# Two collecting PSUM tiles begin without zero products, and the order of all engines is made anew

## The chip, the cores and the metric

The kernel runs on one core of one Trainium2 chip. The core has TensorE (products into PSUM, with weights loaded ahead of each product), VectorE, ScalarE and POOL (GpSimd), and queues that issue DMAs from SyncE, ScalarE and POOL. The metric is the device time of one execution in microseconds (us); less is better. Before the change it was 365.63 us, the median of 3 runs (365.37 to 367.65).

## The reference

`x` is 2048 x 512. A branch `a` takes the real two-dimensional FFT of `x`, multiplies by a complex filter and transforms back. A branch `b` is a dense layer with GELU and 1792 inner features. A gate for each row mixes them:

```python
g = sigmoid((x * gate_w).sum(-1, keepdims=True))
a = irfft2(rfft2(x) * (w_r + 1j * w_i))
b = gelu(x @ w1 + b1) @ w2 + b2
return g * a + (1 - g) * b
```

## The kernel before

All arithmetic is float32; a product that needs the full width is made of three: both operands are split into a high part and a low rest, and high x high, high x low and low x high are added in PSUM (`prods`).

The rows are dealt into four groups of 512, called columns 0 to 3. The FFT branch runs as a forward half (`forward`: TensorE folds, products pd with the table cf, then products py), radix-4 steps along the rows on VectorE (`stage1`, `filt`, `stage4`), the filter (products m with the table wf, in `filt`), and an inverse half (`inverse`: products pz, then pa). The dense branch works on the first half of the columns (`CA`, function `mlp`) as it stands: for each of 14 blocks of inner features, up products into a PSUM tile ph, GELU and a split into high and low part g on ScalarE and VectorE, then down products into po.

The second half of the columns (`CB`, function `fast`) uses a scheme with fewer products. It takes two blocks of features and two columns as a 2 x 2 product of matrices and forms it with seven combined products (function `times`, six matmuls each) in place of eight. Two of the four results are formed in PSUM tiles N, which are new for each pair of blocks. The others pass through the two collecting tiles X[0] and X[1] (ux0 and ux1 in the profile), which are made once and stay for the whole second half. ScalarE copies N[0] into X[0] (`copy`, line 1191), `times(X[0], ...)` then adds onto what stands there, and X[1] is filled by a copy of X[0] in the same way. The products that add onto X never carry the flag that starts an accumulation; before the change, one product of zeros with that flag was made into each collecting tile ahead of the first copy (lines 1166 to 1171).

What runs when is settled by a planner in the kernel file (class `Graph`). Every piece of work is a step: an engine, a cost, the buffers that it reads and writes, and a rank. `add` finds the dependencies; `schedule` plays the steps through time with the written costs, and whenever an engine is free it takes, of the steps whose inputs are there, the one with the lowest rank for which tiles are free. Tiles come from pools of fixed size (PSUM: two pools of four banks, `pf` and `pm`; SBUF: `w` with 46 tiles, `t2k` with 7, `ttab` with 3), tiles of one class are handed out in the order in which the steps were created, and some classes have a ceiling (`most`). The result is one fixed order of instructions for each engine and DMA queue; on the chip each engine runs its own list in that order and waits on semaphores for the others. The ranks are a list of numbers, `RANKS`, one for each step in the order of creation:

```python
ranks = RANKS.split()
assert len(ranks) == len(g.steps)
for s, r in zip(g.steps, ranks):
    s.rank = 0.05 * int(r)
order = g.schedule()
```

Names used below: xf, w, eo, pd, cf, py, zb (forward half); wf, m, y, b0..b3 and c0..c3 with d, s, u (radix steps and filter; y is the spectrum in place); pz, pa, od, u, v (inverse half); ph, g, po, o (dense branch, first half); nu, ux, five, g, poB, oB (second half; nu are the tiles N); wa, wb, ws are first- and second-layer weights, a trailing h or l is the high or low part. `bacc` in device memory collects the dense result: ScalarE takes a po tile out into o, and POOL issues DMAs that add it to bacc.

Line 507 is the helper that issues matmuls, line 1185 the matmuls of `times`, line 498 POOL's adding DMAs and line 558 the low parts of g.

Of the kernel before, what the change touches and what calls it, by code (L numbers as in the profile page):

```python
# [11 lines left out]
F32 = mybir.dt.float32  # L12
# [420 lines left out]
def tile_kernel(ctx: ExitStack, tc: tile.TileContext, xt, xc, w1, w2, b1, b2, x0g, wf, wrev, out, consts):  # L433
# [72 lines left out]
    def mm(ps, w, x, start, stop):  # L506
        pe.matmul(ps, w, x, start=start, stop=stop)  # L507
# [653 lines left out]
    def fast(p):  # L1161
# [4 lines left out]
        if p == 0:  # L1166
# [3 lines left out]
            for x in free["X"]:  # L1170
                m(lambda x=x: mm(x.ap(), zero.ap(), bcast(zero.ap(), 4), True, True), 512, 1, [zero], [x])
# [206 lines left out]
```

## Time and profile before

The profiled execution took 368.04 us of its own, with a span of 366.2 us from its first to its last instruction.

| | us | share of the span |
|---|---|---|
| median of 3 runs | 365.63 | |
| profiled execution | 368.04 | |
| its span | 366.2 | |
| VectorE (DVE) busy | 327.8 | 90% |
| ScalarE (ACT) busy | 256.7 | 70% |
| POOL busy | 69.6 | 19% |

TensorE is PE in the profile, its weight loads PEld. Matmuls are pipelined and the end of each is modelled, so the records of neighbours overlap; the distance from one start to the next is the time that a product holds the engine. TensorE's granted clock averaged 0.999 of full speed.

The share of the 16 DMA engines that were busy, and what they moved, in 40 equal slices of the span:

```profile
DMA  7999785647885937999999943339887637799896
GB/s 224 306 322 303 253 233 166 106 149 233 206 204 129 189 58 155 273 263 365 196 153 217 264 85 117 86 122 225 126 141 150 100 64 156 173 296 241 199 250 184
```

### The profile page before, as it was taken

How to read it: one execution, taken by the hardware profiler on the slowest of the kernel's cores; microseconds unless marked ns; L12 is line 12 of the kernel's file. 1: busy time of each engine (PE TensorE's matmuls, PEld its weight loads, DVE VectorE, ACT ScalarE, POOL GpSimd, SP SyncE). 2: the span in 40 equal slices, each digit the busy share in tenths (PEclk: the TensorE clock that was granted, in tenths of full speed). 3: DMA queues.
4: the chain of work that ended last, by engine and by line, in shares of the span. 5: the costliest groups of instructions: out<-in, count | busy, mean ns of one | idle time of the engine just before them, and what ended most of it. 6: DMA issues, size and time to landing. Idle time of an engine off the chain costs nothing.

```text
span 366.2 us, 5746 instructions
## 1 busy us (share of the span) xinstructions
PE 358.7 (98%) x1808; PEld 302.9 (83%) x1808; DVE 327.8 (90%) x746; ACT 256.7 (70%) x471; POOL 69.6 (19%) x89
## 2 busy tenths in 40 slices
PE   8999999999999999999999999999999999999994
PEld 8888898898878778878888788888888888888884
DVE  5999988998759999899999999999999769899962
ACT  4985778789986241753759975999999998655200
POOL 0210001100211311410333100002333112121220
PEclk9999999999999999999999999999999999999999
DMA  7999785647885937999999943339887637799896
GB/s 224 306 322 303 253 233 166 106 149 233 206 204 129 189 58 155 273 263 365 196 153 217 264 85 117 86 122 225 126 141 150 100 64 156 173 296 241 199 250 184
DMA packets 46719, 70.35 MB, mean 192 GB/s; under 512 B 5600, under 2 KB 19424, under 8 KB 46688
## 3 DMA queue, kind: packets, MB, share of 16 engines
q1 hardware_dynamic: 34880, 48.93, 41.8%
q0 software_dynamic: 11376, 20.71, 35.3%
q10 hardware_dynamic: 432, 0.33, 0.3%
q8 instruction: 14, 0.23, 0.3%
q14 instruction: 17, 0.14, 0.1%
HBM read 48.32 MB, written 19.41 MB: 185 GB/s over the span
## 4 chain that ended last, share of the span: by engine, by line
PE 75%; DVE 12%; DMA 5%; ACT 4%; issue 2%; SPq 1%; DVEq 0%; ACTq 0%
PE poB L507 20%; PE po L507 13%; PE ph L507 11%; PE ux L1185 9%; PE nu L1185 7%; PE pd L507 4%; PE pz L507 3%; PE py L507 3%; PE pa L507 3%; DVE m L856 3%; DMA wf<-in_wf 3%; DMA y<-ownr 1%; DMA xf<-in_xt 1%; DVE y L760 1%; DVE y L758 1%
## 5 line engine op out<-in xcount | busy, mean ns | idle before, releaser
L995 ACT ACTIVATE ph<-ph,b1t 128x512 f32<-128x512 f32 x28 | 18.4, 658 | 25.5 <-PE ph L507 25.2
L498 POOL DMA_DIRECT2D bacc<-o x16 | 15.3, 1029 | 43.2 <-ACT o L1073 43.2
L894 ACT ACTIVATE sw<-y,al 64x512 f32<-64x512 f32 x32 | 22.8, 718 | 0.6
L498 POOL DMA_DIRECT2D bacc<-oB x16 | 13.9, 889 | 43.0 <-ACT oB L1073 33.7
L856 DVE TENSOR_TENSOR m<-y,wf 128x514 f32<-128x514 f32 x32 | 20.7, 688 | 0.0
L507 PE MATMUL pd<-cf,w 128*128 128x129 f32 x128 | 17.7, 276 | 0.0
L507 PEld LDWEIGHTS pz<-tg,pq 128*128 128x128 f32 x128 | 16.8, 191 | 1.1
L507 PEld LDWEIGHTS pd<-cf,w 128*128 128x128 f32 x128 | 16.6, 191 | 1.2 <-DVE zb L698 0.3
L1185 PE MATMUL nu<-xf,wa0h 128*128 128x512 f32 x56 | 17.3, 390 | 0.0
L507 PE MATMUL pz<-tg,pq 128*128 128x128 f32 x128 | 17.2, 274 | 0.0
L507 PE MATMUL py<-zb,tf 128*128 128x258 f32 x96 | 17.1, 295 | 0.0
L723 ACT ACTIVATE y<-pys 64x257 f32<-64x257 f32 x32 | 13.2, 417 | 3.9 <-DVE pys L720 3.4
L507 PE MATMUL pa<-zb,ci 128*128 128x256 f32 x96 | 15.2, 285 | 0.2 <-ACT od L935 0.2
L507 PEld LDWEIGHTS pa<-zb,ci 128*128 128x128 f32 x96 | 13.8, 189 | 1.9 <-ACT od L935 0.7
L507 PEld LDWEIGHTS py<-zb,tf 128*128 128x128 f32 x96 | 14.1, 190 | 1.2 <-ACT pys L716 0.2
L1073 ACT ACTIVATE o<-po 128x512 f32<-128x512 f32 x16 | 9.2, 593 | 8.3 <-PE po L507 8.2
L901 DVE SCALAR_TENSOR_TENSOR pq<-y,al,sw 128x256 f32<-128x256 f32 x32 | 14.4, 479 | 0.0
L695 ACT ACTIVATE zb<-pd 128x256 fp32r<-128x256 f32 x32 | 11.6, 384 | 3.9 <-PE py L507 3.9
L698 DVE TENSOR_TENSOR zb<-pd,zb 128x256 fp32r<-128x256 f32 x32 | 12.5, 417 | 1.1 <-ACT zb L695 1.1
L665 DVE TENSOR_TENSOR w<-eo 128x256 f32<-128x256 f32 x32 | 12.8, 418 | 0.0
L662 DVE TENSOR_TENSOR eo<-xf 128x256 f32<-128x256 f32 x32 | 12.4, 419 | 0.0
L1185 PEld LDWEIGHTS nu<-xf,wa0h 128*128 128x128 f32 x56 | 10.5, 188 | 2.2
(701 smaller groups left out, 1274.3 us busy)
## 6 DMA issues: line engine op xcount, KB each, us to landing
wf<-in_wf SPq DMA_DIRECT2D x16, 257.0 KB, 4.7
bacc<-o POOLq DMA_DIRECT2D x16, 256.0 KB, 6.1
bacc<-oB POOLq DMA_DIRECT2D x16, 256.0 KB, 4.9
xf<-in_xt SPq DMA_DIRECT2D x14, 256.0 KB, 5.0
wr<-in_w SPq DMA_DIRECT2D x14, 256.0 KB, 4.9
tf<-tf SPq DMA_DIRECT2D x16, 192.0 KB, 2.8
bacc<-o SPq DMA_DIRECT2D x8, 256.0 KB, 3.2
ba<-bacc SPq DMA_DIRECT2D x8, 256.0 KB, 4.1
```

Of the source, the lines that this page charges most:

```text
L498: return add("pool", 2.3 * kb / 340, 3.4, lambda: nc.gpsimd.dma_start(dst(), src(), accum_op=ALU.add), reads, writes, rank)
L507: pe.matmul(ps, w, x, start=start, stop=stop)
L662: v(lambda s=s, op=op: vec.tensor_tensor(eo.ap()[:, s], x.ap()[:, 0:2], x.ap()[:, 2:4], op=op), 256, [x], [(eo, s)], feed)
L665: v(lambda s=s, op=op: vec.tensor_tensor(w.ap()[:, s], eo.ap()[:, :, 0], eo.ap()[:, :, 1], op=op), 256, [eo], [(w, s)], feed)
L695: a(lambda c=c: act.activation(segs(xh, c), both(c), AF.Copy), 256, [ps[c]], [(xh, c)], 0)
L698: v(lambda c=c: vec.tensor_tensor(segs(xl, c), both(c), segs(xh, c), op=ALU.subtract), 256, [ps[c], (xh, c)], [(xl, c)], 0)
L723: a(lambda o=o, i=i: act.activation(Y[j].ap()[o:o + HP, 1], pys.ap()[i:i + HP, 1], AF.Copy), 257, [(pys, 1)], [(Y[j], 1 + k)], 0, more=0.1)
L856: v(lambda mk=mk, k=k, y=y, w=w: vec.tensor_tensor(mk.ap(), y.ap(), w.ap()[:, k:k + 1, :ND].to_broadcast([P, 2, ND]), op=ALU.mult), 514, [ ...
L894: a(lambda sw=sw, y=y, o=o, i=i: act.activation(sw.ap()[o:o + HP], y.ap()[i:i + HP, ::-1, :HD], AF.Copy, scale=al.ap()[i:i + HP, 0:1]), 51 ...
L901: v(lambda sw=sw, pq_=pq_, y=y, j=j, k=k, op=op: vec.scalar_tensor_tensor(pq_.ap()[:, k], y.ap()[:, k, :HD], al.ap()[:, 1 + j:2 + j], sw.a ...
L995: a(lambda: act.activation(ps.ap(), ps.ap(), AF.Gelu_apprx_tanh, bias=b1t.ap()[:, f:f + 1]), 600, [b1t], [ps]).table = "gelu"
L1185: pe.matmul(o.ap(), w(wi, e), FX[j].ap()[:, xi, e], start=first, stop=k == 5, skip_group_check=not start)
```

## The change

The tile of zeros, its fill on VectorE and the two products into the collecting tiles are removed. The first access to X[0] and X[1] is now the copy by ScalarE, and the products that add onto them are as before. With three steps fewer (2013 in place of 2016) the list of ranks has a new length, and all its numbers are new. Nothing else differs: costs, pools, ceilings and the other steps are the same.

```diff
 RANKS = """
-0 12 294 321 326 399 330 333 323 340 343 1 13 7 14 20 23 11 35 26 10 2 5 8 19 4 32 56 47 53 78 22 42 73 43 45 21 25 72
...
-2003 2005 2004 2009 2008 2010 2006 2015
+24 7 37 65 66 76 80 81 82 86 72 4 16 3 18 27 0 14 56 43 6 13 10 1 5 12 40 47 93 21 91 42 71 92 70 28 17 32 118 108 106
...
+2008 2009 2010 2011 2012
 """
...
         late = [] if p else [free[CA[1]]]
         if p == 0:
             free["X"] = [buf("pm", [P, 512], F32, f"ux{k}", pool=pp, cls=f"ux{k}") for k in range(2)]
-            zero = buf("w", [P, P], F32R, "zerob", cls="zero")
-            add("vec", 0.3, 0.1, lambda: vec.memset(zero.ap().bitcast(F32), 0.0), [free[CA[1]]], [zero])
-            for x in free["X"]:
-                m(lambda x=x: mm(x.ap(), zero.ap(), bcast(zero.ap(), 4), True, True), 512, 1, [zero], [x])
         X = free["X"]
```

152 rows, old and new, of the table RANKS are left out of this document.

## The prediction

> **What bounds the kernel now.** The page comes first, for the busy shares; then the chain of waits, for what ends last; then the busy time by stretches, for where TensorE is ever idle.
>
> ```profile
> span 366.2 us, 5746 instructions
> PE 358.7 (98%) x1808; PEld 302.9 (83%) x1808; DVE 327.8 (90%) x746; ACT 256.7 (70%) x471; POOL 69.6 (19%) x89
> PE 75%; DVE 12%; DMA 5%; ACT 4%; issue 2%; SPq 1%; DVEq 0%; ACTq 0%
> ```
>
> TensorE is busy for 358.7 of 366.2 us and carries 75% of the chain. The stretches say where the rest is (first number after the stretch is its length, then TensorE, weight loads, VectorE):
>
> ```profile
> 0.00:13.40 13.40, 11.70 (x66) 10.77 (x67) 8.75 (x26) 8.07 (x15) 2.35 (x12) 1.00 0.82 267
> 13.40:101.00 87.60, 87.58 (x491) 75.41 (x489) 79.72 (x217) 72.12 (x154) 9.52 (x11) 1.00 0.79 221
> 101.00:164.70 63.70, 62.82 (x274) 50.69 (x273) 57.78 (x119) 33.05 (x56) 14.98 (x17) 1.00 0.81 181
> 164.70:205.00 40.30, 40.30 (x178) 33.23 (x179) 39.82 (x83) 27.50 (x52) 12.23 (x14) 1.00 1.02 236
> 361.50:366.30 4.80, 0.00 (x0) 0.00 (x0) 0.42 (x1) 0.00 (x0) 0.00 (x0) 0.90 0.51 149
> ```
>
> Before 13.4 us TensorE waits for the first loads; from 361.5 on it has finished and the last output leaves. Between these, its idle time is 0.02 us up to 101, then 0.88 us in the stretch to 164.7 where VectorE does the filter, and 0 in the stretch where the removed products stand. So the sum of the products sets the time, and what an order can win is small. How small follows from the chain's pieces, which give the spacing of products without a wait (start, us, what):
>
> ```profile
> 183.79 4.99 PE po L507 x22
> 188.78 0.23 PE ux L507
> 189.68 1.36 PE nu L1185 x6
> 191.72 0.23 PE ux L507
> ```
> ```profile
> 36.69 0.89 PE pd L507 x8
> 37.58 0.72 PE py L507 x6
> 242.57 0.89 PE pz L507 x8
> 322.66 0.71 PE pa L507 x6
> ```
> ```profile
> L507 PE MATMUL pd<-cf,w 128*128 128x129 f32 x128 | 17.7, 276 | 0.0
> L507 PE MATMUL pz<-tg,pq 128*128 128x128 f32 x128 | 17.2, 274 | 0.0
> L507 PE MATMUL py<-zb,tf 128*128 128x258 f32 x96 | 17.1, 295 | 0.0
> L507 PE MATMUL pa<-zb,ci 128*128 128x256 f32 x96 | 15.2, 285 | 0.2 <-ACT od L935 0.2
> 5.28 0.52 PE L507 MATMUL ph<-mxh,wa0h 128*128 128x128 f32 x2
> ```
>
> A product of 512 columns takes a sixth of 1.36 us, 0.227. By the loops there are 336 each of up, down and second-half down, and 7 pairs x 7 x 6 = 294 of the combined up: 1302, or 295.2 us. The 128 + 128 short ones at 0.89/8 are 28.5 us, the 96 + 96 at 0.72/6 and 0.71/6 are 22.9. Together 346.6 us. From the first real product (5.28) to the end of products (361.5) lie 356.2 us; less 346.6 and the two zero products' 0.46, 9.1 us are bubbles. That is all that any order of the same work can take out before the tail, and part of it belongs to the first loads.
>
> **The zero products.** Removed are one fill on VectorE and two products:
>
> ```profile
> L507 PE MATMUL ux<-zerob x2: 389/389/389, 188.6 to 191.6; 128*128 128x512 f32 x2
> L1169 DVE MEMSET zerob<- x1: 165/165/165, 187.6 to 187.6; 128x128 f32 x1
>   ACT ux L1191: 0.9, 1
> ```
>
> The recorded 389 ns overlap with the next product; on the chain each holds 0.23 us (at 188.78 and 191.72), TensorE is idle for nothing in that stretch, so both come out whole: 2 x 0.227 = **-0.45 us**. The bound on the other side is 0, if the next product then waits; the last row speaks against that: the copy into the first collecting tile waited 0.9 us for the zero product, so it moves forward too. The Trainium skill (TensorE: Matmul & The Clock Gate, Back-to-back issue gap) gives about 131 ns for a product of 512 columns in a stream of loads and products; by it the two would be worth 0.26 us. The chain's 0.227 decides here. The fill is 0.165 us on VectorE, which was busy for 39.82 of 40.30 us there but off the chain: 0, at most -0.17. The two collecting banks (of the pool of four) are taken at the first copy instead of at the zero product, some 3 to 4 us later. No TensorE wait in that stretch names a bank, so 0.
>
> **The order.** The new list is again one rank for each step. I laid it against the places that the steps had on their engine: 481 TensorE steps (the start's zero fills left out) move by 2.2 places on average, at most 40; 745 of VectorE by 4.3, at most 38; 471 of ScalarE by 2.7; 222 of SyncE by 1.1, at most 9; 79 of POOL by 0.8. The old list, for scale, misses the order that ran by 0.6 place on TensorE. A rank far ahead only means "as soon as it can", since a step waits for its inputs and tiles of a class are given out in turn. So it is a shuffle within a few us everywhere, and no work crosses a stage. Three places can be priced.
>
> First, the head. On SyncE the two loads of the forward table, cf, fall three issues back, behind two second-layer weights and the small rev, the second also behind two first-layer weights.
>
> ```profile
> 6.88 0.43 SPq L602 DMA_DIRECT2D cf<-cf  x1
> 7.83 0.64 SPq L984 DMA_DIRECT2D war<-in_w  x1
> cf<-cf SPq DMA_DIRECT2D x2, 129.0 KB, 4.7
> 12.84 0.20 DVE L622 COPY cf<-g 128x4 f32<-128x4 f32 x1
> L507 PE MATMUL pd<-cf,w x128: 271/275/378, 13.5 to 81.4; 128*128 128x129 f32 x128
> ```
>
> At 0.43 to 0.64 us an issue the second goes out at 8.2 to 8.8 and lands 4.7 later, at 12.9 to 13.5; with the 0.20 of the copy behind it the first pd product could start at 13.1 to 13.7, against 13.5 now, when the up products ahead of it are done. Every product behind it in TensorE's queue would wait with it. I take **+0.1**, bounds -0.4 (the weights that now come sooner) and +1 (a load that lands later than its median).
>
> Second, the filter stretch, whose end is a hand-over from VectorE to TensorE:
>
> ```profile
> 163.93 0.68 DVE L558 TENSOR_TENSOR g_10l<-ph,g_10h 128x512 fp32r<-128x512 f32 x1
> 164.66 0.50 PE L507 MATMUL ph<-mxh,wa12h 128*128 128x512 f32 x1 [0.51 <-DVE g_10l L558]
> L856 DVE TENSOR_TENSOR m<-y,wf 128x514 f32<-128x514 f32 x32 | 20.7, 688 | 0.0
> 165.80 0.41 DVE L860 TENSOR_TENSOR y<-m,m 128x257 f32<-128x257 f32 x1
> ```
>
> The filter products m run at a mean of 688 ns. In the new list this g_10l split follows one more step of the kind at 165.80 and two more radix steps of that width (0.41 each), but leaves one m behind it: 1.23 - 0.69, about +0.5 on VectorE. On TensorE one po group of three (0.68) moves ahead of the ph products whose result g_10l splits, and one stays between them as now. The 0.51 wait becomes 0.3 to 1.0, by whether that 0.68 counts. I take 0, since the split's own input moves too.
>
> Third, the tail. Now the last four steps finish the left half of the last tile; in the new list its right half is last, and that half leaves in two 64 KB pieces from two queues.
>
> ```profile
> 360.81 0.49 DVE L1259 TENSOR_TENSOR oB<-y,poB 128x128 f32<-128x128 f32 x2 [0.74 <-PE poB L507]
> 361.52 0.42 DVE L1266 TENSOR_TENSOR oB<-y,poB 128x256 f32<-128x256 f32 x1 [0.23 <-PE poB L507]
> ```
>
> Two subtractions of 0.49 together stand for one of 0.42, the first of two issues can follow the first of them, and the last transfer halves: **-0.2**, bounds -0.6 and +0.2.
>
> For the remaining bubbles I take 0: the same loops make the same hand-overs, the shuffle has no direction that I can read. Bounds: -2.5 (a quarter of the 9.1) and +3 (a third more).
>
> Sum: -0.45 + 0.1 - 0.2 = -0.55 us. The profiled execution took 368.04 of its own, 1.84 more than its span, and would come to 367.5; the median of the three runs lies 2.41 below that execution, at 365.63, so the time is **365.1 us**.
>
> **Rivals.** *Faster by over 1%* (1%, 3.66 us, is about what a measurement of this kernel tells from no change; the edges are 361.97 and 369.29). The new order takes out a third of the bubbles: with the -0.55 it needs 3.1 of 9.1 us, about 361.5. For it: VectorE and TensorE are tied for 164 us, and one better hand-over helps both. Against it: TensorE's named waits are few,
>
> ```profile
> PE ph L507 <- ACT mxh L650: 0.6, 1, 0.6
> PE ph L507 <- DVE g_10l L558: 0.5, 1, 0.5
> PE ph L507 <- DVE g_6l L558: 0.3, 1, 0.3
> ```
>
> 1.4 us in the three longest after the fills; the rest must be many small bubbles. Chance 0.09.
>
> *Slower.* One more filter table late in the filter stretch. These loads stand in SyncE's queue until VectorE gives their slot back, and one is on the chain at its full length:
>
> ```profile
> 142.67 5.00 DMA wf<-in_wf
> DVE wf L851 <- DMA wf<-in_wf: 3.5, 3, 2.1
> ```
>
> Three such waits cost VectorE 3.5 us, the longest 2.1, because it finds other work. A further one costs 2.1 so covered and 5.0 bare, and TensorE, with 0.88 us of idle time in 63.7, has no room to hide it: 367.2 to 370.1, over the edge once more than 4.2 of the 5.0 is bare. For it: VectorE's steps move most, up to 38 places. Against it: SyncE's loads of that stretch keep their places to within one or two. Chance 0.15 for over 1%, with other late waits of that size priced alike.
>
> *The change does less than it says*: the product after a removed one waits instead, and the time is 365.6. That is inside the forecast's band and its range.
>
> **Numbers.** Within 1%: 0.76, of which I see somewhat more below 365.63 than above. My forecast's own bounds are 365.1 less 3.1 and plus 4: I set 362.2 to 369.9, which leaves out most of the faster rival and the far part of the slower one.
>
> **What would show it.** No ux product with zerob, and the chain from 183 to 200 without the two 0.23 pieces; 1806 products in place of 1808. TensorE's idle time between 13.4 and 361.5 still near 1 us (7.5 of the span, less 1.70 before and 4.80 after); the first pd product within 0.5 us of 13.5; the filter stretch ending within 1 us of 164.7 less whatever the head shifts; the end of products to the end of the span at 4.6 rather than 4.8. The forecast is wrong if one TensorE wait of over 2 us appears, or if the wait for wf grows beyond 3.5 us together with it.

## The result, and the profile after

The changed kernel takes **368.53 us** (median of 22 runs, 366.93 to 373.28) against 366.88 us of the kernel before on the same chip (22 runs, 365.24 to 374.22): ratio **1.0062, 95% interval 1.0043 to 1.0081**. It is slower by 0.6%, 2.3 us by this ratio, where I forecast 0.55 us less. (The two medians lie 1.65 us apart; the interval allows 1.6 to 3.0 us.) It stays within 1%, and 368.53 lies in the range; the direction is wrong. The three runs that I started from (365.63) lay 1.25 us below the median of the 22.

The page of the profiled execution, with the lines that answer to those of before:

```profile
span 368.4 us, 5714 instructions
PE 359.0 (97%) x1806; PEld 301.9 (82%) x1806; DVE 328.7 (89%) x745; ACT 256.4 (70%) x471; POOL 69.9 (19%) x89
PE 50%; DVE 20%; DMA 12%; ACT 12%; issue 3%; SPq 2%; DVEq 0%
```

Two products and one fill are gone. TensorE now holds half of the chain of waits in place of three quarters; VectorE, ScalarE and the transfers hold the rest. The same stretches of the busy times as before, with one from 270 to 340 us (after the stretch its length, then TensorE, weight loads, VectorE, ScalarE, GpSimd, granted clock, DMA share, GB/s):

```profile
0.00:13.40 13.40, 11.20 (x64) 10.42 (x65) 8.68 (x27) 7.96 (x15) 1.88 (x12) 1.00 0.86 265
13.40:101.00 87.60, 85.87 (x485) 74.25 (x484) 79.94 (x214) 70.44 (x152) 9.38 (x12) 1.00 0.77 219
101.00:164.70 63.70, 63.47 (x279) 51.59 (x278) 57.44 (x119) 33.65 (x56) 15.64 (x18) 1.00 0.81 178
164.70:205.00 40.30, 40.30 (x179) 33.16 (x177) 39.99 (x83) 28.63 (x52) 12.32 (x14) 1.00 1.00 247
270.00:340.00 70.00, 69.19 (x368) 58.89 (x367) 59.21 (x126) 55.55 (x95) 15.78 (x18) 1.00 0.73 152
364.30:368.40 4.10, 0.02 (x1) 0.00 (x0) 0.48 (x2) 0.00 (x0) 0.00 (x0) 1.00 0.43 137
```

In before the stretch from 270 to 340 us was:

```profile
270.00:340.00 70.00, 70.00 (x378) 60.37 (x377) 61.36 (x132) 55.69 (x96) 16.25 (x19) 1.00 0.76 167
```

Idle time of TensorE has come up in two stretches: 1.73 us from 13.4 to 101 and 0.81 between 270 and 340, where before had 0.02 and 0. In the filter stretch, from 101 to 164.7, it has gone down from 0.88 to 0.23. TensorE's waits name the two largest (line, releaser: us in total, times, longest):

```profile
PE ph L507 <- ACT pys L716: 1.3, 1, 1.3
PE nu L1181 <- DVE v L946: 0.6, 1, 0.6
```

From this one pair of profiles I would have told a simple story: 1.5 us at 28 us, 0.8 at 276. Experiments on both, and a second profile of each kernel, showed that it isn't the story of the 2.3 us.

### The profile page after: what moved, and what is told of

The parts are those of the page before. It is cut to its first block, busy times and chain, and to the rows that moved or that the text cites. A ratio compares the mean times of both kernels' runs of the same rounds, so it can differ in the third digit from the quotient of the medians.

```text
span 368.4 us, 5714 instructions
## 1 busy us (share of the span) xinstructions
PE 359.0 (97%) x1806; PEld 301.9 (82%) x1806; DVE 328.7 (89%) x745; ACT 256.4 (70%) x471; POOL 69.9 (19%) x89
## 4 chain that ended last, share of the span: by engine, by line
PE 50%; DVE 20%; DMA 12%; ACT 12%; issue 3%; SPq 2%; DVEq 0%
PE poB L507 15%; PE ux L1181 6%; PE ph L507 6%; PE po L507 6%; PE nu L1181 5%; DMA wf<-in_wf 4%; DVE m L856 4%; PE pz L507 3%; PE py L507 3%; DMA xf<-in_xt 3%; PE pa L507 3%; PE pd L507 3%; ACT sw L894 2%; DVE y L760 2%; DMA xb010xe<-in_xc 2%
## 5 line engine op out<-in xcount | busy, mean ns | idle before, releaser
L507 PEld LDWEIGHTS pa<-zb,ci 128*128 128x128 f32 x96 | 13.5, 188 | 2.2 <-ACT od L935 0.6
L507 PE MATMUL pa<-zb,ci 128*128 128x256 f32 x96 | 14.4, 283 | 0.3
```

## The experiments

All ratios are to the kernel before, over runs on the same chip. Steps are named by tile, and a moved step keeps its inputs ahead of it.

**The removal alone**, in the order of before:

```diff
-            add("vec", 0.3, 0.1, lambda: vec.memset(zero.ap().bitcast(F32), 0.0), [free[CA[1]]], [zero])
+            add("vec", 0.3, 0.1, lambda: None, [free[CA[1]]], [zero])
...
-                m(lambda x=x: mm(x.ap(), zero.ap(), bcast(zero.ap(), 4), True, True), 512, 1, [zero], [x])
+                m(lambda: None, 512, 1, [zero], [x])
```

> The order of before, with the fill and the two zero products left out and nothing else moved. Theory (the removal is worth what the chain gave, the order costs the rest): 0.45 us faster than before, ratio 0.9988, 1806 products, the chain near 189 us without the two pieces of 0.23. Rival A (the next product waits in their place): ratio 1.000 and a new wait of about 0.2 us near 189 us. Rival B (the accumulation without them is itself what costs, through collecting banks held otherwise): slower than before, ratio up to 1.006 as the whole change.

Measured: 367.46 against 366.44 us, 1.0021 (0.999 to 1.0051). No gain; the 0.9988 of the theory is just outside.

**The same with the new tail** (the last left half ahead of the right half):

```diff
     order = g.schedule()
+    for ns, to in (((2004, 2005), 2003), ((2006,), 2005), ((2007,), 2006)):
+        for n in ns:
+            order.remove(g.steps[n])
+        k = order.index(g.steps[to]) + 1
+        order[k:k] = [g.steps[n] for n in ns]
```

> The order of before without the zero products, and with the last tile's halves finished in the new kernel's order: the left half of 256 columns first, the right half of two 128s, which leaves in two pieces, last. Theory (both parts of the change that I priced as gains are gains, and the tail is worth the 0.73 us that the trace of after shows): from the last product to the end of the span 4.0 us in place of 4.8, and 1.2 us faster than before, ratio 0.9968. Rival (the shorter tail of the profile of after is one execution's transfer time): ratio 0.9988 as without the tail, with 4.6 us or more from the last product to the end.

Measured: 367.16 us, 1.0028 (1.0001 to 1.0054). Neither gain came (the profile has 3.75 us from the last product to the end, but the time does not show it). The profile of this second kernel, its VectorE and then its TensorE, shows why the removal gave none (start us, us, what, in brackets idle time and its releaser):

```profile
199.24 1.29 DVE L856 TENSOR_TENSOR m<-y,wf 128x514 f32<-128x514 f32 x2
201.60 0.17 DVE L851 SCALAR_TENSOR_TENSOR wf<-wf,rev 128x4 f32<-128x4 f32 x1 [1.07 <-DMA wf<-in_wf]
201.68 0.68 DVE L558 TENSOR_TENSOR g_0l<-ux,g_0h 128x512 fp32r<-128x512 f32 x1
202.88 0.68 DVE L558 TENSOR_TENSOR g_1l<-nu,g_1h 128x512 fp32r<-128x512 f32 x1
```
```profile
203.28 0.39 PE L507 MATMUL poB<-g_1h,wb1hb 128*128 128x512 f32 x1
204.42 0.50 PE L507 MATMUL poB<-g_1l,wb1hb 128*128 128x512 f32 x1 [0.76 <-DVE g_1l L558]
```

TensorE is early, but VectorE stands for 1.07 us on the last filter table, with the splits g_0l and g_1l queued behind it. TensorE gives back at 203 us what it won at 189. In the new order the table's first use stands behind the splits (the second profile of the changed kernel):

```profile
199.55 0.69 DVE L558 TENSOR_TENSOR g_0l<-ux,g_0h 128x512 fp32r<-128x512 f32 x1
201.02 0.68 DVE L558 TENSOR_TENSOR g_1l<-nu,g_1h 128x512 fp32r<-128x512 f32 x1
202.59 0.15 DVE L851 SCALAR_TENSOR_TENSOR wf<-wf,rev 128x4 f32<-128x4 f32 x1
```

**That use put behind the splits in the old order too**: the first edit, and in the list `(((1073, 1074), 1338),)`.

> The order of before without the zero products, and with VectorE's first use of the last filter table (the edge step of wf15 and the first product with it) put behind the three splits g_0l, g_1l, g_1l that TensorE waits for. Theory (without the zero products TensorE reaches those splits sooner, but VectorE stands before them on the last filter table, 8 to 9 us from issue to landing): the wait of TensorE for g_1l near 203 us is gone, the removed products are worth their 0.45 us, ratio 0.999. Rival (the removal is lost for another reason, or the splits then wait for ScalarE): ratio 1.002, as with the products left out alone.

Measured: 366.81 against 366.36 us, 1.0012 (0.9992 to 1.0031). The theory's 0.999 is just outside. The wait for the filter table is gone, and the next table stands in its place:

```profile
200.89 0.69 DVE L558 TENSOR_TENSOR g_1l<-nu,g_1h 128x512 fp32r<-128x512 f32 x1 [0.32 <-ACT g_1h L557]
202.39 0.29 DVE L888 TENSOR_TENSOR tg<-tg,gb 128x128 f32<-128x128 f32 x1 [0.81 <-DMA tg<-ti]
202.60 0.68 DVE L558 TENSOR_TENSOR g_1l<-ux,g_1h 128x512 fp32r<-128x512 f32 x1
```

TensorE still waits 0.45 us there. The wait on a load ahead of the splits is shown; that the removal would be worth 0.45 us without any such wait is not.

**The two large waits of the changed kernel**, each taken away by moving one or two steps: `(((220,), 92),)` puts ScalarE's split of xf13 behind the copy pys0 and one cosine copy; `(((1838, 1198), 1162),)` puts VectorE's watl5 and pq7 behind the two reads of bank pa211.

> The kernel after, with one ScalarE step put back: the split of xf13 goes behind the copy pys0 and one cosine copy zb1, six places. Theory (ScalarE's queue stands behind a late load, and the copy that would free a PSUM bank stands behind that): the wait of about 1.3 to 1.5 us of the first-layer product ph at 28.6 us shrinks to about 0.3, and the time is 1.2 us below the kernel after, so about 1.1 above before, ratio to before 1.003. Rival (the x loads are late and TensorE then waits for the split itself, or for another bank): the wait moves on by a few us with its size kept, ratio to before 1.006.

> The kernel after, with two VectorE steps (the small half of table watl5 and a product pq7) put behind the two reads u21, v21 of PSUM bank pa211. Theory (the bank comes free too late because VectorE does other work first): the wait of the product nu50 at 276 us falls from 0.6 or more to 0.2 or less, the lag behind before that grows by 0.8 us near 276 us does not, and the time is 0.8 us below the kernel after, ratio to before 1.004. Rival (VectorE is short of time there as a whole, so that the two steps put back delay the next split by as much): the gain is 0.3 us or less, and a wait of TensorE for g2_8l or another result shows within 3 us of it.

Measured: 1.0048 (1.002 to 1.0077) and 1.0052 (1.0028 to 1.0076). Both are a little below the kernel after, and neither difference is outside its uncertainty, so the times decide neither theory against its rival. In the profiles the wait is gone: that of the first has none for pys, that of the second none at 276 us. How such a wait comes about is read from the profile of the kernel after. This chain (start us, us, what) ends in the wait at 28 us:

```profile
18.97 10.35 DMA xf<-in_xt
...
29.34 0.63 ACT mxh L650
29.97 0.28 ACT pys L716
...
30.30 3.02 PE ph L507 x12
```

An x load takes 10.35 us, ScalarE's split waits for it, and the copy that frees a PSUM bank is queued behind that split. In the same profile VectorE did two other things at 274.87 and 275.47 while the bank's two readers were due:

```profile
274.87 0.68 DVE L1139 TENSOR_TENSOR watl<-wr,wath 128x512 fp32r<-128x512 f32 x1
275.47 0.48 DVE L901 SCALAR_TENSOR_TENSOR pq<-y,al,sw 128x256 f32<-128x256 f32 x1
275.86 0.68 DVE L945 TENSOR_TENSOR u<-pa,od 128x512 f32<-128x512 f32 x1
276.46 0.68 DVE L946 TENSOR_TENSOR v<-pa,od 128x512 f32<-128x512 f32 x1
```

But these waits are not there at this size in every execution, as the next two runs show; so one profile without them does not show that the moved step took them away.

**Both kernels again, unchanged.**

> The kernel before itself, as a control: ratio 1.000 within 0.003. Single profiles of these kernels differ by up to 2 us, so a second profile is to show which of before's waits return. Theory (the removal alone gave nothing because the last filter table, 8 to 9 us from issue to use, is what the end of the filter work waits for): that load is again used within 0.5 us of its landing, and TensorE waits for nothing near 203 us. Rival: it lands with 2 us to spare, and the wait at 203 us without the zero products has another cause.

> The kernel after itself, as a control: ratio 1.006 within 0.003. Theory (the wait of 1.5 us at 28.6 us comes from a late x load ahead of the bank's copy in ScalarE's queue, and the load's landing differs from execution to execution): the wait at 28.6 us is anywhere from 0.2 to 1.5 us, and the wait for v21 near 276 us is there again with 0.6 to 0.9. Rival (both are fixed by the order): both return at the same size.

Measured: 1.0004 (0.9984 to 1.0023) and 1.0061 (1.0038 to 1.0084). The profile of the kernel after now has a span of 365.1 us in place of 368.4, with no wait for pys and 0.25 us in place of 0.8 near 276; that of before has 366.3 again. So the two second profiles say "faster" while the runs say 0.6% slower. In the second profile of before VectorE again used the last filter table without a wait, 8.4 us after its issue (194.3 to 202.7), and TensorE had no wait near 203 us; the record has no landing for that load, so how much it had to spare isn't known. Single profiles can't place 2 us here; from now on the order is cut and timed.

**Orders spliced by stage.** Each kernel has the code of after, without zero products (the one with zero products has the code of before). Its list is made of both orders, and the planner then leaves all but 4 to 57 of some 2,000 steps at that place on their engine, the others at most 6 places off:

```diff
-    s.rank = 0.05 * (rank in the new list)
+    s.rank = 0.05 * (place in: first K steps of one order, then the other steps as the other order has them)
```

First a cut at K = 700, about 101 us:

> Without the zero products; the first 700 steps (to about 101 us) in the order of before, the rest in the order of after. Theory A (most of the loss is made in the first 100 us, where the trace of after falls 1.6 us behind): ratio 1.001 to 1.002, and the profile shows no wait of over 0.3 us for pys. Theory B (most is made after 205 us, where it falls 1.5 to 2.8 behind): ratio 1.006, and the waits near 255, 276, 330 us return.

> Without the zero products; the first 700 steps in the order of after, the rest in the order of before. Theory A (the loss is in the first 100 us): ratio 1.006, at least 1 us slower than the order of before without zero products. Theory B (the loss is made after 205 us): ratio 1.002, as the order of before without zero products gave.

Measured: 1.0124 (1.008 to 1.0169) and 1.008 (1.0054 to 1.0106). Both are slower than either parent: a cut at the start of the filter stretch costs more than what it should tell apart (the profile of the first has waits of 2.2 and 1.5 us of TensorE for VectorE's splits g_6l and g_12l there). Inconclusive, and a warning that a seam, the place where the two orders meet, has a price of its own. Then K = 1203, in the second half (by the products, at about 212 us rather than 215):

> The kernel before with its zero products; the first 1203 steps (to about 215 us) in its own order, the rest in the order of after. Theory (the new order loses its time in many small hand-overs after 215 us; over the traces so far 0.9 to 2.2 us, on average 1.4): 1.4 us slower than before, ratio 1.004, with waits of 0.2 to 0.8 us near 247, 252, 257, 276 and 286 us. Rival (the loss of after is made earlier, by late loads that the single profiles happened not to show): ratio 1.000 within 0.002.

> The kernel after (no zero products); the first 1203 steps in its own order, the rest in the order of before. Theory: 1.4 us faster than after, ratio to before 1.002, and from 215 us to the last product the same excess over the products' own time as in the profile of before. Rival: ratio 1.006, as after.

Measured: 1.0069 (1.004 to 1.0097) and **0.9994 (0.997 to 1.0018)**. This is the decisive pair. The new order behind 212 us alone makes the old kernel as slow as the changed one, with whatever the seam costs in it; the old order there takes the whole loss away although the zero products are gone. The rival (loss earlier) falls. The size is more than my theory's 1.4 us: against the kernel after (1.0061) it is 2.4 us, uncertain by some 1.2. Cuts at 251 and 274 us follow:

> As the kernel with the new order up to 212 us and the old one behind it (ratio 0.999), but with the new order kept up to its step 1434, about 251 us. Theory (the loss of 2.4 us is spread over the half in many small hand-overs): about 0.6 us of it lies here, ratio 1.001. Rival (one place, 251 to 285 us): ratio 0.999.

> The new order up to its step 1554, about 274 us, the old one behind. Theory (spread): 1.2 to 1.5 us of the loss, ratio 1.003. Rival (one place): most of the loss, ratio 1.005 or more.

> The new order, with the old one put between its steps 1203 and 1554, about 212 to 274 us. Theory (spread): 0.9 to 1.2 us of the loss is left, ratio 1.002 to 1.003. Rival (one place, mostly before 274 us): ratio 1.000.

Measured: 1.004 (1.002 to 1.0059), 1.0014 (0.9995 to 1.0033), 1.0042 (1.0023 to 1.0061). The first is out of line: it has less of the new order than the second and is 1 us slower. A seam's price would explain it; that is not shown. The other two agree with each other, and their rival (one place, ahead of 274 us) lies outside both intervals. From 274 us on, the new order costs 1.0061 - 1.0014, 1.7 us, behind the new order, and 1.0042 - 0.9994, 1.8 us, behind the old one. From 212 to 274 it costs 0.7 us in both pairs. Each difference is uncertain by some 1 us. Last, a cut at 343 us:

> As the kernel with the old order behind 212 us (ratio 0.999), but with the last 100 steps, from about 343 us to the end, in the new order. Theory (the end of the kernel: transfers crowd behind the last products): 1.0 us or more of the loss, ratio 1.002 to 1.004, and 4.4 us or more from the last product to the end. Rival (TensorE's waits between 274 and 343 us): ratio 0.999 to 1.000.

> The new order up to about 343 us, the old one for the last 100 steps. Theory (the end): ratio 1.002 to 1.003, 1.0 us or more below after. Rival (274 to 343 us): ratio 1.005 to 1.006, as after.

Measured: 0.9999 (0.9983 to 1.0014) and 1.0089 (1.0064 to 1.0115). The end costs nothing: my theory there falls, and the rival holds. (The second is 1 us above the kernel after; its profile has 1.6 us of the wait for pys.)

**The new order's first half, the old second half, and the split put back**, run twice:

> The new order up to 212 us, the old one behind, no zero products, and ScalarE's split of xf13 put behind the copy pys0 and one cosine copy. Theory: the wait for pys near 28 us (0.5 to 1.5 us in the profiles) is gone and 0.5 us is won over the same order without the move, ratio 0.998, below both kernels. Rival (the wait only moves to the next product that needs a split): ratio 0.999 to 1.000, as without the move.

> The same kernel as e19 (no zero products, the new order up to 212 us with one split moved back, the old order behind): ratio 0.998 within 0.002 again, if the 0.7 us that the first 12 runs showed is real; 0.9995, as without the moved split, if it was chance.

Measured: 366.11 against 366.83 us, **0.9981 (0.9961 to 1.0002)**, and 365.71 against 366.11, **0.9978 (0.9964 to 0.9992)**. This one beats both kernels, by 0.2% over before; both profiles are without a wait for pys.

**What the new order does behind 212 us.** The chain from 274 to 343 us, in the kernel with the old second half and in the second profile of the kernel after:

```profile
by line: PE poB L504 41.2%; PE ux L1178 20.5%; PE pz L504 15.5%; PE nu L1178 12.0%; PE pa L504 11.0%
```
```profile
by line: PE poB L507 35.8%; PE ux L1181 15.9%; PE pz L507 12.9%; DMA wb8lb_raw<-in_w 11.8%; PE pa L507 9.7%; PE nu L1181 8.0%; ACT ux L995 1.8%; ACT zb L913 1.5%; DVE g_9l L558 1.0%; ACT wb8hb L969 0.9%; ACT wb9lb L563 0.9%; ACT wb9hb L969 
```

In this profile of the old order it is TensorE alone. In that of the new one it runs through a weight load, ScalarE and VectorE until 286 us (the pieces, and what the old order has at the same time):

```profile
283.80 0.56 ACT wb9hb L969
284.38 0.63 ACT wb9lb L563
285.01 0.49 ACT g_9h L557
...
285.53 0.70 DVE g_9l L558
...
286.27 0.99 PE pa L507 x6
```
```profile
283.20 1.38 PE poB L504 x6
284.57 0.72 PE pa L504 x6
285.29 0.89 PE pz L504 x8
286.18 0.69 PE poB L504 x3
```

ScalarE makes both halves of a weight table (wb9) before it splits g_9, and the profile puts 0.32 us of TensorE's idle time, ahead of six products pa, down to VectorE's half of that split (by their names these products don't read it). ScalarE stands in that chain ahead of 291 us in seven of the eight profiles with the new order there, and in none of the twelve with the old one; one of the twelve, of the kernel with the split put back, has ScalarE, VectorE and a load in it from 297 to 319 us. Between 212 and 274 us the largest of several small waits in the second profile of the kernel after is for a transfer. The small half of wb4 is completed by an adding transfer of GpSimd:

```profile
245.55 6.65 DMA wb4lb<-in_w
252.21 0.04 issue
252.25 1.20 PE poB L507 x4
```

It lands at 252.21 and TensorE takes it at 252.25. The same transfer in the kernel with the old second half, and the product that uses it:

```profile
245.82 0.86 POOL L495 DMA_DIRECT2D wb4lb<-in_w  x1 [18.59 <-PE nu L1178]
DMA to landing us min/median/max: 4.6/4.6/4.6
252.56 0.39 PE L504 MATMUL poB<-g_4h,wb4lb 128*128 128x512 f32 x1
```

It lands 2.2 us before its use. In all nine profiles with the new order around it, TensorE takes wb4's half within 0.15 us of its landing; in all eleven with the old one it lies ready for 2.0 to 2.3 us. The use has not moved: it comes 6.4 to 6.8 us behind GpSimd's issue in all twenty. The landing has: 6.3 to 6.7 us behind the issue in the new order, 4.5 to 4.8 in the old. In the new order SyncE issues the loads wr and wb6lb_raw 0.7 and 1.1 us behind it, in the old one 3.7 us behind and 0.4 us ahead; that these loads slow it down is likely, but no run moved them alone. A transfer that was covered has become one that TensorE can wait for; in the nine profiles the wait is 0.0 to 0.3 us.

## Why the prediction was right and wrong

To lay profiles of different orders against each other, I counted each TensorE product at the spacing of the prediction (0.227 per 512 columns, 0.111 and 0.118 for the short ones) and took the rest of the time as waiting. The zero products don't count as work, so their 0.45 us stand in the 0.77. By stretches of equal work, in us, mean and range over the profiles of one order there (for the last two rows, of one order from 274 to 343 us; the row from 226 us leaves out the two kernels cut at 101 us):

```
stretch (us)               old order               new order
 16 to  65                 1.21 (0.96-1.47, n=7)   1.89 (1.24-3.13, n=10); split put back 1.31 (1.24-1.38, n=3)
183 to 210                 0.77 with zero products (0.75-0.81, n=3)
                           1.04 without (0.88-1.28, n=4)   0.48 (0.41-0.62, n=13)
226 to 277                 0.81 (0.76-0.98, n=9)   1.56 (1.31-2.29, n=6)
277 to 335                 0.70 (0.38-1.56, n=12)  0.98 (0.75-1.36, n=8)
last product to the end    4.10 (3.64-4.76, n=12)  4.51 (3.98-4.97, n=8)
```

**What bounds it.** Right: TensorE's sum of products sets the time, and the loss of 2.3 us lies inside the bounds that I gave its bubbles (-2.5 and +3).

**The zero products, -0.45.** Half right. They are gone, 1806 for 1808, and the stretch around them has 0.3 us less in the new order. In the old order the removal alone won nothing. "Both come out whole" failed there: VectorE was busy for 39.8 of 40.3 us, and I called that "off the chain". It was off by less than the 0.45 us; the last filter table decided when TensorE could go on. The chain after still has six products in 1.36 us, so the 0.227 holds, and what failed was not the price but the place. The Trainium skill (TensorE: Matmul & The Clock Gate, Back-to-back issue gap) with its 131 ns would have given 0.26 us; the trace does not agree. That taking the two banks later changes nothing was right; no wait of TensorE in that stretch names them.

**The head, +0.1.** The first pd product starts at 13.6 and 13.1 us in the two profiles, within 0.5 of 13.5 as said. But the price of the head isn't there. It is the split of xf13 that moved ahead of pys0 on ScalarE: 0.6 us between 16 and 65 us on average (1.89 against 1.31), anywhere from 0 to 1.9. I followed the moved loads on SyncE, not the moved waits on ScalarE.

**The filter stretch, 0, and my rival there.** The wait for g_10l, which I left at its size, is gone: it stands in six of the seven profiles with the old order there (0.15 to 1.13 us) and in none of the thirteen with the new one. By the count above, the stretch from 65 to 165 us has 2.8 us of waiting in the old order (1.6 to 4.1, n=5) and 1.6 in the new one (1.1 to 2.2, n=12; the two kernels cut at 101 us and the profile of the removal alone, with one wait of 4.1 us there, are left out). So the shuffle won some 1.2 us where I took 0. No further filter table came late in the kernel after: that rival did not happen. What happened is its mechanism, a load in front of VectorE's splits, in the kernels where I took the products out of the old order.

**The tail, -0.2.** Nothing that the runs can tell. With the new end alone the ratio is 0.9999, with the old one 0.9994, and the last product to the end takes 3.6 to 5.0 us in all profiles. I took a spread between executions, of which I had one, for a size.

**The remaining bubbles, 0.** This is the step that failed. "The shuffle has no direction that I can read": it had one, and not the same everywhere. Behind 212 us it costs 2.4 us by the runs (1.0061 against 0.9994), 0.7 of it up to 274 us; ahead of that, what it won in the filter stretch covers what it lost near 28 us. My signs of being wrong did not see it: in neither profile of the kernel after is a wait of TensorE over 2 us (the longest has 1.3), and in the first the wait for wf fell from 3.5 to 2.3 us. The loss is in waits each smaller than that. That a term of 0 was too bold could have been seen in the profile of before, from ScalarE's share in the second half and the slack of each load (from landing to first use), which the prediction leaves out:

```profile
245.00:265.00 20.00, 19.77 (x106) 16.69 (x104) 19.53 (x42) 19.63 (x35) 6.12 (x7) 1.00 0.81 169
265.00:285.00 20.00, 20.00 (x106) 17.08 (x105) 19.20 (x42) 19.73 (x37) 6.99 (x8) 1.00 0.80 142
```

In before, from 245 to 285 us, TensorE is busy for 39.8 of 40 us, VectorE for 38.7 and ScalarE for 39.4. With three engines tied, an order tuned to these hand-overs has, I think, more to lose than to win by a shuffle of a few places; that is an argument, and the filter stretch, where the shuffle won, is against making it a rule. I saw one tie (VectorE and TensorE, 164 us) and took it for a reason on both sides.

**What stays open.** The profiles show about 1.5 us of the 2.4 (from 210 us to the end, mean 7.4 us of waiting and tail in seven profiles against 5.9 in ten). Between 274 and 343 us they show some 0.3 us on TensorE and 0.4 at the end where the runs say 1.7, uncertain by 1. Later transfers in executions that were not profiled may fill that gap, or the uncertainty of the runs; no run here decides. That ScalarE's halving of wb9 is the cause at 286 us, and SyncE's two loads at 252 us, is argued from the profiles; moving them was not tried.

## What to carry to other kernels

Where several engines are busy for nearly all of a stretch (here 97 to 99% of 40 us), ask of a new order not how far steps move but what each in-order queue now has in front of the step that the bound engine waits for, above all a step that waits for a transfer. List the slack of every load before and after: where 2 us became 0, as here, each later landing is a wait of the bound engine, even if the profiles at hand show only 0.0 to 0.3 us of it. And before you place 2 us by comparing two profiles, take a second profile of each, or splice the two orders at stage ends and time them, with the price of a seam in mind.

## What the runs showed that I had not expected

- Two executions of the same kernel after had spans of 368.4 and 365.1 us at a granted clock of 1.00; the x load of 256 KB ahead of the late split took 10.35 us to land in the first and 8.80 in the second. The 256 KB of wb4 that GpSimd adds took 6.65 us in the second of these and 4.57 in the kernel with the old second half. The Trainium skill (DMA: Bandwidth & Descriptors, Anatomy of one DMA) gives 2.0 us and the bytes at 436 GB/s for a transfer that GpSimd issues, 2.6 us for 256 KB by my estimate. The measurement decides: a schedule that counts on 2.6 us would take wb4's to land 2 to 4 us too early.
- After a wait TensorE loses a little more than the wait. The first product after it is recorded with 0.50 us in place of 0.39, and the next starts 0.34 us behind it in place of 0.23:

```profile
28.34 0.39 PE L507 MATMUL po<-g_2l,wb2h 128*128 128x512 f32 x1
28.57 0.40 PE L507 MATMUL po<-g_2h,wb2l 128*128 128x512 f32 x1
30.30 0.50 PE L507 MATMUL ph<-mxh,wa4h 128*128 128x512 f32 x1 [1.33 <-ACT pys L716]
30.64 0.39 PE L507 MATMUL ph<-mxl,wa4h 128*128 128x512 f32 x1
```

The next start is 0.33 to 0.34 us behind in 36 of the 38 waits of over 0.15 us that stand ahead of two products of 512 columns, after the first 13 us, in the twenty profiles. So many short waits cost 0.11 us each on top of their sum.
